# A transformer block on one core: the first half's attention begins in the product stage, and three additions change their engine

## The chip, the core and the metric

The kernel runs on one core of a Trainium2 chip. A core has several engines that run side by side, each strictly in the order of its own program: TensorE (PE, matrix products, with PEld for the loading of its weights), VectorE (DVE), ScalarE (ACT), GpSimd (POOL), and SyncE (SP), whose queue issues the transfers (DMA) between main memory and the on-chip memory SBUF. PE writes its results into PSUM, from where DVE and ACT take them. The metric is the time of one execution in microseconds of the device, as the median of several runs.

## The reference

The block adds three things: the input, a local attention on its layer norm, and a dense layer pair with the Mish function on the same layer norm. There are 2048 tokens of width 576, 32 heads of width 18, a window of 8 keys at a distance of 2 tokens each, and a hidden width of 4608.

```python
def block(x, wqkv, wo, w1, b1, w2):          # S=2048, D=576, F=4608, H=32, Dh=18
    xn = layernorm(x)
    q, k, v = split_heads(xn @ wqkv)
    idx = pos[:, None] - 2 * arange(8)[None, :]        # keys at t, t-2, ..., t-14
    logits = einsum("bhsd,bhswd->bhsw", q, k[idx]) * Dh ** -0.5
    attn = softmax(where(idx >= 0, logits, -1e9))
    o = einsum("bhsw,bhswd->bhsd", attn, v[idx])
    h = xn @ w1 + b1
    return x + o @ wo + (h * tanh(softplus(h))) @ w2
```

## The kernel before

The tokens are worked on in two halves of 1024 (hf = 0 and 1). Every operand of a matrix product is split into a high part and a low part (a cast, then a subtraction), and each product is three matmuls: high by high, high by low and low by high. Weights and activations also go through sums and differences of blocks, so that seven block products do the work of eight (names such as T1 to T4, S1 to S4, B11 to B22, P1 to P7 are such blocks and products).

The order of PE is written out as a list of items, called the plan; an item's position in it is its slot. The first half runs: the first part of the query, key and value products (items `q`, matmuls L540), then the rest of them in seven-product form (items `y`, L649, slots 20 to 32), then 18 quads of the dense layers: `m` items (L902 and L908: hidden layer h, blocks c11, c21, c22) and `p` items (L1004: second layer, added by DVE into `acc`, L1008). The second half has the items `v` and `z` (L649) in the place of `y`, then quads whose second layer is in part a seven-product scheme (L1096; its activations u are sums of stored blocks, its weights pw are fetched by `p_fetch`, L1064; DVE adds PSUM into accP, L1102, and `p_join`, L1105, joins two such sums), in part direct (L1117, with DVE's additions L1120). At the end come the items `o`, the product with wo (L1300).

All other work is put into slots by `before(slot, fn)`, and the engines' own order follows from it. Four tables correct this placing: `MOVED` moves the n-th call of `before` by some slots, to before or behind the item's own work; `STEPS` has the slots of the attention's steps, for each half; `SUMS` puts certain reductions of the attention into slots of their own; `AHEAD` names slots whose held Mish work runs first.

The attention of a half is a generator, eight rounds of two units (of two heads each). A round: POOL multiplies queries and keys (`pr`, L764, two instructions of 128x576 for each of four parts), DVE reduces each part to logits L (L769), DVE and ACT do the softmax (the exponential with a load of ACT's function table, L790; Mish, L948, uses another table), POOL multiplies with the values (`pv`, L803), DVE reduces (`og`, L809) and transposes (oT, L830), and SP stores the result (o_d, L839). Keys, values and queries are read back from main memory (kv_d, q_d) by `load_kv` and `load_kq`: the generator issues the first loads 4 slots ahead of the first step of the first half.

Tiles of one tag share a number of buffers. The tag `kv` has four: the key and value tiles of the attention, and in the stage `y` also the queries that this stage collects. A tile can be written only when the last reader of the buffer's former tile is done.

For the first product with wo, POOL forms the sums T3, T1, T2 and T4 (`wo_sum`, L1243, T2 from T1, T4 from T2), ACT casts their high parts and DVE subtracts (L1201, tiles raw_T and woh_T) for the low parts of T3, T1 and T2.

Of the kernel before, what the change touches and what calls it, by code (L numbers as in the profile page):

```python
# [12 lines left out]
ALU = mybir.AluOpType  # L13
# [22 lines left out]
MOVED = {0: (-1, 1),  # L36
 38: (-2, 1),
 41: (0, 0),
 47: (2, 1),
 49: (-2, 1),  # L40
 98: (-1, 1),
 108: (2, 0),
 117: (1, 0),
 118: (0, 0),
 121: (-2, 0),
 122: (1, 1),
 123: (0, 1, 0),
 126: (0, 1, 0),
 128: (0, 0),
 131: (0, 1, 0),  # L50
 135: (0, 1, 0),
 138: (0, 0),
 143: (0, 0),
 144: (0, 0),
 217: (0, 0),
 234: (0, 0),
 238: (-2, 1),
 282: (0, 0),
 345: (0, 0),
 378: (1, 1),  # L60
 389: (1, 0),
 400: (0, 0),
 413: (1, 1),
 416: (0, 0),
 421: (-1, 1),
# [3 lines left out]
 433: (0, 0),  # L69
 442: (2, 1),  # L70
 446: (0, 0),
 447: (0, 0),
 452: (-1, 1),
 465: (2, 1),
 468: (1, 1),
 481: (0, 1, 0),
 489: (0, 0),
 529: (0, 0),
 535: (0, 0),
 609: (1, 0),  # L80
 611: (0, 1, 0),
 614: (-1, 1, 0),
 618: (-2, 0),
 622: (-1, 1),
 625: (1, 1),
# [4 lines left out]
 662: (-2, 1),  # L90
 671: (2, 1),
 694: (1, 1),
 695: (-2, 1),
 737: (-1, 1),
 765: (2, 1),
 771: (1, 1),
 777: (1, 1),
 794: (0, 0),
 802: (0, 0),
 806: (0, 0),  # L100
 811: (-2, 0),
 834: (0, 0),
# [9 lines left out]
 1006: (0, 0),  # L112
 1042: (0, 0),
 1046: (2, 1),
 1056: (0, 1, 0),
 1057: (0, 0),
 1068: (0, 0),
 1070: (-2, 0),
 1086: (2, 1),
 1095: (1, 1),  # L120
 1101: (2, 1),
 1104: (2, 1),
 1106: (0, 0),
 1107: (2, 1),
 1116: (0, 0),
 1121: (0, 0),
 1122: (1, 0),
 1160: (-2, 1),
 1161: (-3, 1),
 1164: (1, 1),  # L130
 1166: (-2, 1),
 1201: (0, 1, 0),
 1207: (0, 0),
 1208: (0, 0),
 1212: (-2, 1),
 1219: (2, 1),
 1221: (1, 1),
# [5 lines left out]
 1237: (0, 0),  # L143
 1248: (0, 0),
 1249: (0, 0),
 1250: (0, 0),
 1251: (-2, 1),
 1253: (0, 0),
 1263: (2, 1),
 1266: (-2, 1),  # L150
 1274: (0, 1, 0),
 1292: (0, 0),
 1298: (1, 1),
 1336: (0, 0),
# [4 lines left out]
STEPS = ((33, 36, 47, 49, 53, 57, 63, 67, 70, 77, 78, 83, 85, 91, 95, 98, 105, 107, 111, 117, 123, 127, 130, 137, 139, 143,  # L159
# [7 lines left out]
SUMS = {(0, 0): (42, 1),  # L167
 (0, 1): (38, 0),
 (0, 11): (86, 0),
 (0, 15): (101, 0),  # L170
 (0, 17): (110, 0),
 (0, 32): (171, 0),
 (0, 34): (176, 0),
 (0, 36): (180, 0),
 (0, 37): (186, 0),
 (0, 38): (190, 0),
 (0, 47): (213, 1),
 (0, 50): (230, 0),
 (0, 53): (233, 1),
 (1, 2): (259, 1),  # L180
 (1, 5): (264, 0),
 (1, 6): (267, 0),
 (1, 8): (273, 0),
 (1, 10): (276, 0),
 (1, 28): (321, 0),
 (1, 35): (337, 0),
 (1, 38): (343, 0),
 (1, 46): (366, 0),
 (1, 47): (371, 0),
 (1, 50): (379, 1),  # L190
 (1, 54): (389, 0),
 (1, 56): (394, 1)}
AHEAD = (35, 37, 39, 42, 80, 84, 171, 184, 190, 191, 201, 218, 230, 231, 232, 237, 238, 240, 298, 315, 317, 336, 337, 357,
 391, 413, 414)
# [7 lines left out]
def block_kernel(ctx: ExitStack, tc: tile.TileContext, x, wq, wo, w1, b1, w2, mask, out):  # L202
# [1042 lines left out]
    def wo_src(name):  # L1245
        return (traw if name[0] == "T" else wraw)[name]
# [603 lines left out]
```

## Time and profile before

| quantity | us |
|---|---|
| median of 3 runs | 1100.46 |
| lowest and highest run | 1099.98, 1100.76 |
| the profiled execution | 1099.32 |
| its span, first to last instruction | 1097.5 |
| PE busy | 1085.5 |
| DVE busy | 883.8 |
| POOL busy | 789.6 |
| ACT busy | 512.8 |

All durations come from the one profiled execution, whose own time stands 1.14 us below the median. Of the rows that are shown later: a row of the stretches has the bounds in us, then the busy time and count of PE, PEld, DVE, ACT and POOL, the granted clock of PE, the busy share of the DMA engines, and GB/s. A row of the timeline has start and length in us, then engine, line, operation and tiles (output <- inputs), shapes and count; in brackets the idle time before it and what ended it. A row of the waits has who waited for what: us in all, times, the longest. A row of a line has the shortest, median and longest duration in ns, and the first and last start. In the chain of work that ended last, a row has start and length of one piece.

### The profile page before, as it was taken

Reading aid. Unit: us, or ns where it says so; the run is one execution under the profiler, and the core shown is the slowest. Engines: PE = TensorE matmul, PEld = TensorE weight load, DVE = VectorE, ACT = ScalarE, POOL = GpSimd, SP = SyncE. Lnnn points to the kernel's source line nnn. Section 1 sums busy time; section 2 is a strip of 40 time slices with the busy share of each in tenths; the row PEclk is TensorE's granted clock in tenths of the full one; section 3 lists DMA queues with packets and bytes.
Section 4 is the critical chain, followed back from the end, with each engine's and each line's share of the span. In section 5 each row is a group of like instructions: output and inputs, shape, how many; then the busy total and the mean of one; then the engine's idle time right before and its main releaser. Section 6 shows DMA issues by size and latency. Waiting matters only on the chain.

```text
span 1097.5 us, 18210 instructions
## 1 busy us (share of the span) xinstructions
PE 1085.5 (99%) x6454; PEld 999.2 (91%) x6454; DVE 883.8 (81%) x1469; ACT 512.8 (47%) x947; POOL 789.6 (72%) x635
## 2 busy tenths in 40 slices
PE   9999999999999999999999999999999999989998
PEld 8998899999999999999999888989999999979998
DVE  6775888898888889997976758887887885787886
ACT  5554564454456445455523354444444334244353
POOL 2435867778777787977777768778676799967432
PEclk9999999999999999999999999999999999999999
DMA  6769986877877588785799999675668576487864
GB/s 226 277 229 376 368 309 241 281 252 261 275 248 257 205 293 295 278 299 161 274 298 335 303 346 338 240 239 202 213 219 265 169 245 219 156 305 248 245 221 139
DMA packets 187327, 283.99 MB, mean 259 GB/s; under 512 B 53826, under 2 KB 127844, under 8 KB 187236
## 3 DMA queue, kind: packets, MB, share of 16 engines
q1 hardware_dynamic: 187236, 282.82, 76.0%
q8 instruction: 51, 0.84, 0.3%
q14 instruction: 40, 0.33, 0.1%
HBM read 166.58 MB, written 116.19 MB: 258 GB/s over the span
## 4 chain that ended last, share of the span: by engine, by line
PE 92%; DMA 3%; DVE 2%; issue 1%; ACT 1%; POOL 0%; POOLq 0%; SPq 0%
PE h L902 29%; PE po L1004 21%; PE po L1096 11%; PE po L1117 7%; PE h L908 5%; PE o L1300 5%; PE pq L540 3%; PE y L649 2%; PE z L649 2%; PE v L649 2%; PE zT L649 1%; PE yT L649 1%; DMA pw<-kept_B 1%; DMA pw<-kept_T 1%; DMA vw_T<-kept_vT 1%
## 5 line engine op out<-in xcount | busy, mean ns | idle before, releaser
L1004 PEld LDWEIGHTS po<-w,act 128*128 128x128 f32 x1728 | 236.1, 188 | 6.4 <-DVE acc L1008 1.0
L1004 PE MATMUL po<-w,act 128*128 128x288 f32 x1728 | 240.8, 295 | 0.6 <-DVE acc L1008 0.6
L803 POOL TENSOR_TENSOR pv<-L,kv 128x576 f32<-128x576 f32 x128 | 172.0, 1450 | 42.3 <-DVE L L796 19.8
L764 POOL TENSOR_TENSOR pr<-q,kv 128x576 f32<-128x576 f32 x128 | 195.0, 1552 | 1.9 <-DVE L L769 1.0
L954 POOL TENSOR_TENSOR act<-c,act 128x512 fp32r<-128x512 f32 x69 | 94.5, 1370 | 79.6 <-ACT act L953 78.6
L1096 PEld LDWEIGHTS po<-pw,u 128*128 128x128 f32 x1008 | 137.8, 188 | 6.1 <-issue 2.5
L1096 PE MATMUL po<-pw,u 128*128 128x288 f32 x1008 | 141.0, 295 | 1.3 <-ACT rt L936 0.7
L1008 DVE TENSOR_TENSOR acc<-po,acc 128x288 f32<-128x288 f32 x288 | 117.1, 448 | 18.9 <-PE po L1004 17.3
L902 PE MATMUL h<-xt,t 128*128 128x512 f32 x432 | 111.0, 391 | 0.1
L902 PE MATMUL h<-S,t 128*128 128x512 f32 x432 | 110.6, 391 | 0.1
L948 ACT ACTIVATE c<-c,b1c 128x512 f32<-128x512 f32 x69 | 50.0, 725 | 122.4 <-DVE c L947 122.3
L902 PE MATMUL h<-xt,wa 128*128 128x512 f32 x432 | 104.0, 389 | 0.0
L809 DVE TENSOR_REDUCE og<-pv 128x144 f32<-128x1152 f32 x64 | 86.1, 1345 | 19.6 <-POOL pv L803 19.6
L769 DVE TENSOR_REDUCE L<-pr 128x64 f32<-128x1152 f32 x64 | 85.7, 1341 | 15.7 <-POOL pr L764 15.7
L902 PEld LDWEIGHTS h<-xt,wa 128*128 128x128 f32 x432 | 80.9, 188 | 16.8 <-DMA wa<-kept_wa 0.3
L902 PEld LDWEIGHTS h<-xt,t 128*128 128x128 f32 x432 | 79.0, 188 | 15.4 <-DVE t L450 0.5
L902 PEld LDWEIGHTS h<-S,t 128*128 128x128 f32 x432 | 77.9, 188 | 13.8 <-ACT rm L936 0.4
L1117 PEld LDWEIGHTS po<-w,act 128*128 128x128 f32 x576 | 78.3, 188 | 5.2 <-DVE accP L1120 3.7
L1117 PE MATMUL po<-w,act 128*128 128x288 f32 x576 | 79.6, 295 | 3.3 <-DVE accP L1120 3.3
L1102 DVE TENSOR_TENSOR accP<-po,accP 128x288 f32<-128x288 f32 x156 | 63.2, 448 | 15.9 <-PE po L1096 7.9
L936 ACT COPY c<-h 128x512 f32<-128x512 f32 x69 | 40.4, 586 | 73.0 <-PE h L908 36.9
L947 DVE TENSOR_TENSOR c<-h,c 128x512 f32<-128x512 f32 x69 | 47.1, 683 | 23.9 <-PE h L908 20.7
(305 smaller groups left out, 2081.3 us busy)
## 6 DMA issues: line engine op xcount, KB each, us to landing
kv<-kv_d SPq DMA_DIRECT2D x64, 396.0 KB, 6.1
kept_t<-t SPq DMA_DIRECT2D x36, 512.0 KB, 5.0
t<-kept_t SPq DMA_DIRECT2D x36, 512.0 KB, 4.7
pw<-kept_T SPq DMA_DIRECT2D x24, 576.0 KB, 5.9
rw<-in_w SPq DMA_DIRECT2D x36, 320.0 KB, 5.1
kept_wa<-wa SPq DMA_DIRECT2D x18, 640.0 KB, 4.7
wa<-kept_wa SPq DMA_DIRECT2D x18, 640.0 KB, 7.4
rw<-in_w SPq DMA_DIRECT2D x36, 288.0 KB, 4.5
```

What stands on the lines that cost most here:

```text
L649: nc.tensor.matmul(h, l, r_, start=i == 0 and name in ("B11", "B21", "T3"), stop=i == len(seq) - 1, skip_group_check=True)
L764: nc.gpsimd.tensor_tensor(out=pr[:, x:x + hh], in0=q[:, j0 + x:j0 + x + hh, None, :].to_broadcast([P, hh, W, CU]), in1=win(kt, 0, CU, j0 + ...
L769: nc.vector.tensor_reduce(L[:, k, j0:j0 + hj].rearrange("p j w h -> p (j w h)"), pr.rearrange("p j w (h d) -> p (j w h) d", h=2), axis=AX, ...
L803: nc.gpsimd.tensor_tensor(out=pr[:, x:x + hj].rearrange("p j d w -> p j w d"), in0=L[:, k, x:x + hj, :, h:h + 1].to_broadcast([P, hj, W, DH]),
L809: nc.vector.tensor_reduce(og[:, c0:c0 + DH, :].rearrange("p d j -> p j d"), pr, axis=AX, op=ALU.add)
L902: nc.tensor.matmul(ph, wt[:, wl, wk * P:(wk + 1) * P], X[:, xs, :], start=first and i == 0, stop=last and i == len(seq) - 1, skip_group_ch ...
L954: nc.gpsimd.tensor_tensor(out=a[:, 1, :], in0=t, in1=a[:, 0, :].bitcast(F32), op=ALU.subtract)
L1004: nc.tensor.matmul(po, acts[hf, q, b, j][:, al, tok], done["w2", hf, 2 * q + j][:, wl, c * HC:(c + 1) * HC], start=i == 0, stop=i == 5)
L1008: nc.vector.tensor_tensor(out=t, in0=po, in1=t, op=ALU.add)
L1096: nc.tensor.matmul(po, units[e, k, qq][:, al, tok], w[:, qq, wl, :], start=i == 0, stop=i == 5)
L1102: nc.vector.tensor_tensor(out=t, in0=po, in1=t, op=ALU.add)
L1117: nc.tensor.matmul(po, acts[hf, q, b, j][:, al, tok], done["w2", hf, 2 * q + j][:, wl, c * HC:(c + 1) * HC], start=i == 0, stop=i == 5)
```

## The change

It has four parts.

1. The queries that the stage `y` collects lie in other buffers: two of them in one tile of tag `wa0`, the other two in tags `xn` and `acc`. The four `kv` buffers are free in that stage. `reserve` keeps only `wa1` for the first quad's weights and the tile for those queries.
2. The first half's attention has its first step in slot 26 (in the stage `y`) where it was slot 33, and its last in slot 252 where it was 251.
3. Three operations of POOL are done by DVE: the join P7 += P6 of the first part (`p_join`), and the differences T3 and T2 (`wo_sum`).
4. `MOVED`, `STEPS`, `SUMS` and `AHEAD` have new numbers, in both halves: loads, casts, subtractions, stores and reductions are moved by some slots. PE's own instructions and their order are as before.

```diff
-STEPS = ((33, 36, 47, 49, 53, 57, 63, 67, 70, 77, 78, 83, 85, 91, 95, 98, 105, 107, 111, 117, 123, 127, 130, 137, 139, 143,
+STEPS = ((26, 27, 29, 31, 34, 40, 45, 49, 56, 58, 63, 67, 72, 77, 80, 86, 90, 95, 99, 107, 110, 113, 120, 125, 129, 134, 139,
...
@@ -399,8 +473,8 @@
     def reserve():
-        for i in range(2):
-            early[f"wa{(i + 1) % 2}"] = sb.tile([P, 2, 5 * P], F32R, tag=f"wa{(i + 1) % 2}", bufs=1, name=f"wa_0_{i}")
+        early["wa1"] = sb.tile([P, 2, 5 * P], F32R, tag="wa1", bufs=1, name="wa_0_0")
+        early["qs"] = sb.tile([P, 2, 5 * P], F32, tag="wa0", bufs=1, name="qs_y0")
...
@@ -626,8 +700,13 @@
             if hf:
                 qs = sb.tile([P, 5 * P], F32, tag="xn", bufs=XNB, name=f"qs_{n_}")
+            elif g == 0:
+                if b == 0:
+                    yq["qs"] = early.pop("qs") if "qs" in early else sb.tile([P, 2, 5 * P], F32, tag="wa0", bufs=1, name=f"qs_{n_}")
+                qs = yq["qs"][:, b]
             else:
-                qs = sb.tile([P, (TJ + HALO) * CU], F32, tag="kv", bufs=4, name=f"qs_{n_}")
+                tag = ("xn", "acc")[b]
+                qs = sb.tile([P, (5 * P, D)[b]], F32, tag=tag, bufs=BUFS[tag], name=f"qs_{n_}")
...
@@ -1102,7 +1181,8 @@
     def p_join(a, b, pr):
-        nc.gpsimd.tensor_tensor(out=pacc[a, pr], in0=pacc[a, pr], in1=pacc[b, pr], op=ALU.add)
+        eng = nc.vector if (a, pr) == ("P7", 0) else nc.gpsimd
+        eng.tensor_tensor(out=pacc[a, pr], in0=pacc[a, pr], in1=pacc[b, pr], op=ALU.add)
...
@@ -1240,7 +1320,8 @@
         name, x, y = (("T3", "B22", "B12"), ("T1", "B12", "B11"), ("T2", "B22", "T1"), ("T4", "B21", "T2"))[n]
-        nc.gpsimd.tensor_tensor(out=traw[name], in0=wo_src(x), in1=wo_src(y), op=ALU.subtract)
+        eng = nc.vector if name in ("T3", "T2") else nc.gpsimd
+        eng.tensor_tensor(out=traw[name], in0=wo_src(x), in1=wo_src(y), op=ALU.subtract)
```

The line numbers of the kernel after are some 74 to 81 higher than those before. What the tables do to an engine's order is seen at the following places. A row has line, operation, output <- inputs (a number at a name's end only counts tiles) and the shape; x2 stands for two alike.

DVE in the second half, between the additions of quad 12's and quad 13's second layer (accP <- po, accP), before:

```order
L1120 TENSOR_TENSOR accP3_1_7610<-po_1_12_0_1_1_0_10640,accP3_1_7610 128x288
L1120 TENSOR_TENSOR accP3_1_7610<-po_1_12_0_1_1_1_10648,accP3_1_7610 128x288
L809 TENSOR_REDUCE og_1_5_10491<-pv_1_5_0_1_10564 128x8x18
L947 TENSOR_TENSOR c11_1_14_10673<-h2_1_14_10675,c11_1_14_10673 128x512
L1120 TENSOR_TENSOR accP4_0_7605<-po_1_13_1_0_0_0_10707,accP4_0_7605 128x288
L1120 TENSOR_TENSOR accP4_0_7605<-po_1_13_1_0_0_1_10715,accP4_0_7605 128x288
L1120 TENSOR_TENSOR accP5_0_7607<-po_1_13_1_0_1_0_10723,accP5_0_7607 128x288
L1120 TENSOR_TENSOR accP5_0_7607<-po_1_13_1_0_1_1_10731,accP5_0_7607 128x288
L809 TENSOR_REDUCE og_1_5_10491<-pv_1_5_1_0_10689 128x8x18
```

and after:

```order
L1200 TENSOR_TENSOR accP3_1_7583<-po_1_12_0_1_1_0_10639,accP3_1_7583 128x288
L1200 TENSOR_TENSOR accP3_1_7583<-po_1_12_0_1_1_1_10647,accP3_1_7583 128x288
L1324 TENSOR_TENSOR raw_T3_10660<-rB22_10608,rB12_10444 128x576
L888 TENSOR_REDUCE og_1_5_10490<-pv_1_5_0_1_10563 128x8x18
L1026 TENSOR_TENSOR c11_1_14_10672<-h2_1_14_10674,c11_1_14_10672 128x512
L1200 TENSOR_TENSOR accP4_0_7578<-po_1_13_1_0_0_0_10706,accP4_0_7578 128x288
L1200 TENSOR_TENSOR accP4_0_7578<-po_1_13_1_0_0_1_10714,accP4_0_7578 128x288
L1200 TENSOR_TENSOR accP5_0_7580<-po_1_13_1_0_1_0_10722,accP5_0_7580 128x288
L1200 TENSOR_TENSOR accP5_0_7580<-po_1_13_1_0_1_1_10730,accP5_0_7580 128x288
L888 TENSOR_REDUCE og_1_5_10490<-pv_1_5_1_0_10688 128x8x18
L1324 TENSOR_TENSOR raw_T2_10662<-rB22_10608,raw_T1_10661 128x576
```

The difference T3 (rB22, rB12: blocks of wo) now stands ahead of the reduction `og`, and T2 behind the next one, ahead of the additions that follow it.

DVE a quad later, where the low parts of T3 and T1 are formed, before:

```order
L1120 TENSOR_TENSOR accP3_1_7610<-po_1_13_0_1_1_1_10894,accP3_1_7610 128x288
L769 TENSOR_REDUCE L_1_6_10785<-pr_1_6_0_1_10849 128x64
L1201 TENSOR_TENSOR raw_T3_10661<-raw_T3_10661,woh_T3_10863 128x576
L1201 TENSOR_TENSOR raw_T1_10662<-raw_T1_10662,woh_T1_10923 128x576
L947 TENSOR_TENSOR c11_1_15_10936<-h2_1_15_10938,c11_1_15_10936 128x512
L769 TENSOR_REDUCE L_1_6_10785<-pr_1_6_1_0_10903 128x64
```

and after:

```order
L1200 TENSOR_TENSOR accP3_1_7583<-po_1_13_0_1_1_1_10893,accP3_1_7583 128x288
L1281 TENSOR_TENSOR raw_T3_10660<-raw_T3_10660,woh_T3_10862 128x576
L848 TENSOR_REDUCE L_1_6_10784<-pr_1_6_0_1_10848 128x64
L1281 TENSOR_TENSOR raw_T1_10661<-raw_T1_10661,woh_T1_10947 128x576
L1026 TENSOR_TENSOR c11_1_15_10935<-h2_1_15_10937,c11_1_15_10935 128x512
L848 TENSOR_REDUCE L_1_6_10784<-pr_1_6_1_0_10901 128x64
```

The low part of T3 moves ahead of a reduction of logits; that of T1 stands behind it.

POOL in the stage `y`, where the sums tt of the first quads' w1 (loaded as rw1) are formed, before:

```order
L435 TENSOR_TENSOR tt0_0_1073<-rw1_1_979,rw1_0_977 128x256
L435 TENSOR_TENSOR tt1_0_1074<-rw1_1_979 128x256
L435 TENSOR_TENSOR tt0_0_1073<-rw1_1_979,tt0_0_1073 128x256
L435 TENSOR_TENSOR tt1_0_1074<-rw1_0_977,tt0_0_1073 128x256
L435 TENSOR_TENSOR tt0_1_1177<-rw1_3_1119,rw1_2_1117 128x256
L435 TENSOR_TENSOR tt1_1_1178<-rw1_3_1119 128x256
L435 TENSOR_TENSOR tt0_1_1177<-rw1_3_1119,tt0_1_1177 128x256
L435 TENSOR_TENSOR tt1_1_1178<-rw1_2_1117,tt0_1_1177 128x256
L764 TENSOR_TENSOR pr_0_0_0_0_1210<-q_0_0_1082,kv0_0_0_1080 128x576 x2
L764 TENSOR_TENSOR pr_0_0_0_1_1264<-q_0_0_1082,kv0_0_0_1080 128x576 x2
```

and after:

```order
L843 TENSOR_TENSOR pr_0_0_0_0_1009<-q_0_0_900,kv0_0_0_898 128x576 x2
L843 TENSOR_TENSOR pr_0_0_0_1_1035<-q_0_0_900,kv0_0_0_898 128x576 x2
L509 TENSOR_TENSOR tt0_0_1092<-rw1_1_983,rw1_0_981 128x256
L509 TENSOR_TENSOR tt1_0_1093<-rw1_1_983 128x256
L509 TENSOR_TENSOR tt0_0_1092<-rw1_1_983,tt0_0_1092 128x256
L509 TENSOR_TENSOR tt1_0_1093<-rw1_0_981,tt0_0_1092 128x256
L843 TENSOR_TENSOR pr_0_0_1_0_1099<-q_0_1_904,kv0_0_1_902 128x576 x2
L843 TENSOR_TENSOR pr_0_0_1_1_1161<-q_0_1_904,kv0_0_1_902 128x576 x2
L509 TENSOR_TENSOR tt0_1_1196<-rw1_3_1131,rw1_2_1129 128x256
L509 TENSOR_TENSOR tt1_1_1197<-rw1_3_1131 128x256
```

The first four of the attention's products (x2 each) now stand ahead of and between the sums.

Two further places are told in words. At the end of the first half's products the reduction of L from pr_0_5_1_0 and a subtraction of the other half's layer norm stood on DVE right ahead of the additions into acc of the last quad; they now come behind those. On SP's queue, at the fetches pw of the last seven-product group, pw_5_2 stood ahead of the fetches w2_1_26, wa_1_14, w2_1_27, wc_1_14 and kv1_1_10, and these ahead of pw_5_3; now these five come first, then pw_5_2, the stores of oT, t0_1_14 and pw_5_3. The tiles w2 and pw share four buffers: pw_5_2 now takes that of pw_5_0, which is free when PE is done with it, and w2_1_27 the one that pw_5_2 had. Ahead of the fetch vw_T1 of the item v, two zacc loads (blocks of the kept y weights for the item z) go earlier on SP's queue, and one such pair more comes ahead of the fetch's second part.

More of the change, by code (lines that the diff above doesn't have):

```diff
@@ L77 @@
  489: (0, 0),
+ 499: (-1, 1),
+ 503: (0, 0),
+ 512: (1, 1),
+ 513: (1, 1),
+ 521: (0, 1, 0),
  529: (0, 0),
+ 533: (1, 1),
  535: (0, 0),
+ 545: (1, 1),
+ 565: (0, 0),
+ 603: (-1, 1),
  609: (1, 0),
  611: (0, 1, 0),
- 614: (-1, 1, 0),
- 618: (-2, 0),
+ 614: (-1, 1),
+ 617: (-2, 1),
+ 619: (0, 1, 0),
  622: (-1, 1),
- 625: (1, 1),
+ 623: (-2, 1),
+ 624: (-2, 1),
  627: (2, 1),
@@ L89 @@
  652: (-1, 1),
- 662: (-2, 1),
+ 662: (-2, 0),
  671: (2, 1),
+ 682: (2, 1),
+ 684: (0, 1, 0),
+ 685: (-2, 1),
  694: (1, 1),
  695: (-2, 1),
- 737: (-1, 1),
- 765: (2, 1),
+ 737: (1, 1),
+ 750: (2, 1),
  771: (1, 1),
  777: (1, 1),
+ 782: (0, 1, 0),
+ 787: (0, 1, 0),
+ 791: (0, 0),
+ 793: (0, 0),
  794: (0, 0),
  802: (0, 0),
+ 803: (1, 1),
+ 805: (2, 1),
  806: (0, 0),
+ 810: (-1, 1),
  811: (-2, 0),
+ 812: (0, 1, 0),
  834: (0, 0),
```

137 lines of the change are left out of this document (95 added, 42 removed), and 11 rows, old and new, of the table STEPS.

## The prediction

> **What bounds the kernel now.** I began with the span and clock of the core and the busy times, then asked what TensorE (PE) waits for, then read stretches of the span side by side.
>
> ```profile
> core 0: 1097.5 us, clock 1.000
> PE 1085.5 (99%) x6454; PEld 999.2 (91%) x6454; DVE 883.8 (81%) x1469; ACT 512.8 (47%) x947; POOL 789.6 (72%) x635
> ```
>
> PE is busy for 99% at full clock, and the change leaves its instructions and their order alone. So the time can fall only by PE's waits, and it rises wherever PE must wait anew. The list of PE's waits, longest first:
>
> ```profile
> PE po L1117 <- DVE accP L1120: 3.3, 1, 3.3
> PE warm L227 <- POOL ident masks.py:199: 1.3, 1, 1.3
> PE v L649 <- DMA vw_T<-kept_vT: 1.1, 1, 1.1
> PE po L1096 <- ACT rt L936: 0.7, 1, 0.7
> PE po L1096 <- DMA pw<-kept_T: 0.6, 1, 0.6
> PE po L1004 <- DVE acc L1008: 0.6, 1, 0.6
> ```
>
> Each happens once. The warm start is before anything that changes. By stretches (PE, PEld, DVE, ACT, POOL busy):
>
> ```profile
> 75.00:100.00 25.00, 25.00 (x126) 23.22 (x125) 11.78 (x26) 10.07 (x26) 5.69 (x7) 1.00 1.05 350
> 125.00:500.00 375.00, 375.00 (x2271) 343.56 (x2270) 331.37 (x524) 191.78 (x310) 294.87 (x245) 1.00 0.78 271
> 500.00:600.00 100.00, 98.37 (x574) 93.34 (x574) 78.33 (x135) 42.32 (x106) 75.41 (x64) 1.00 0.82 267
> 600.00:700.00 100.00, 99.21 (x529) 87.19 (x528) 71.36 (x102) 44.05 (x80) 75.20 (x55) 1.00 0.95 318
> 880.00:905.00 25.00, 24.41 (x158) 22.61 (x157) 22.26 (x35) 8.32 (x14) 24.07 (x17) 1.00 0.78 245
> 905.00:940.00 35.00, 35.00 (x221) 32.49 (x221) 20.25 (x39) 13.49 (x20) 34.15 (x28) 1.00 0.60 216
> 940.00:965.00 25.00, 21.73 (x129) 19.44 (x128) 20.94 (x23) 8.87 (x15) 21.63 (x17) 1.00 0.52 146
> ```
>
> In the first half's products (125 to 500 us) PE never stops: nothing is to be gained there, only lost. PE's idle time in the four stretches where it stops is 1.63 + 0.79 + 0.59 + 3.27 = 6.28 us, and that is the most that can come back. Over half of it is one wait, from 960.8 to 964.06 us. What POOL, DVE and PE did there:
>
> ```profile
> 953.58 2.90 POOL L764 TENSOR_TENSOR pr<-q,kv 128x576 f32<-128x576 f32 x2
> 957.60 2.90 POOL L764 TENSOR_TENSOR pr<-q,kv 128x576 f32<-128x576 f32 x2
> 963.86 1.29 POOL L954 TENSOR_TENSOR act<-c,act 128x512 fp32r<-128x512 f32 x1 [3.37 <-ACT act L953]
> ...
> 952.48 1.35 DVE L769 TENSOR_REDUCE L<-pr 128x64 f32<-128x1152 f32 x1 [2.10 <-POOL pr L764]
> 953.75 8.03 DVE L1201 TENSOR_TENSOR raw_T<-raw_T,woh_T 128x576 fp32r<-128x576 f32 x2
> 961.70 0.68 DVE L947 TENSOR_TENSOR c<-h,c 128x512 f32<-128x512 f32 x1
> 963.56 1.53 DVE L1120 TENSOR_TENSOR accP<-po,accP 128x288 f32<-128x288 f32 x4
> ...
> 964.06 2.23 PE L1117 MATMUL po<-w,act 128*128 128x288 f32 x15 [3.27 <-DVE accP L1120]
> L1201 DVE TENSOR_TENSOR raw_T<-raw_T,woh_T x4: 744/1256/7362, 953.7 to 974.7; 128x576 fp32r<-128x576 f32 x4
> ```
>
> The pair of L1201 took 8.03 us, the one of them 7.362 us where the shortest of that line took 0.744. Its two inputs lie in SBUF, as POOL's do, and it ended just after POOL fell idle, at 957.60 + 2.90 = 960.50. So DVE was kept out for 6.6 us while POOL ran instruction after instruction; behind it stood the accP additions that empty PSUM for PE. POOL itself is the cause: 34.15 of 35 us busy before 940.
>
> **The change, part by part.** *Three additions go from POOL to DVE* (the P7 join and the differences T3 and T2). T3 and T2 come off POOL in its full stretch:
>
> ```profile
> L1243 POOL TENSOR_TENSOR raw_T<-rB,rB x2: 1448/1456/1465, 931.2 to 936.2; 128x576 f32<-128x576 f32 x2
> L1243 POOL TENSOR_TENSOR raw_T<-rB,raw_T x2: 1517/1520/1524, 941.3 to 946.9; 128x576 f32<-128x576 f32 x2
> 910.27 0.46 DVE L1120 TENSOR_TENSOR accP<-po,accP 128x288 f32<-128x288 f32 x1 [2.53 <-PE po L1117]
> 928.03 1.35 DVE L809 TENSOR_REDUCE og<-pv 128x144 f32<-128x1152 f32 x1
> 930.91 0.69 DVE L947 TENSOR_TENSOR c<-h,c 128x512 f32<-128x512 f32 x1 [1.53 <-PE h L908]
> 937.53 0.46 DVE L1120 TENSOR_TENSOR accP<-po,accP 128x288 f32<-128x288 f32 x1 [0.44 <-PE po L1117]
> ```
>
> POOL loses T3 (1.45) and T2 (1.52), and a join of the same size (about 1.45, an estimate from these): 4.4 us. DVE gains three instructions that no row shows on it. The nearest row is L1201: same shape and two inputs in SBUF, 0.744 at best, 1.256 the median, 7.362 at worst. I take 1.3 each. The join stands ahead of the 2.53 us gap before 910.27, T3 ahead of the reduce of 928.03 and so of the 1.53 us gap before 930.91: both are covered. T2 stands behind the next og reduce and right before the accP additions of 937.53, where the gap is 0.44, so those run about 0.9 us late. PE has room for that: of the 6.6 us for which DVE was held up at 953.75, PE paid 3.27, so the first 3.3 us of such a delay were free. T2 also waits for T1 on POOL, which two removed instructions bring forward. Cost of the three on PE: 0, from 0 to the starvation priced below.
>
> The gain is the 3.27 at 960.8. With 4.4 us less ahead of it POOL is done with its row of pr products earlier, but I do not expect it to idle much before: its rows carry over 3 us of backlog (3.37 of idle came only once ACT was the one waited for). What decides is whether the L1201 addition gets its turn; in the changed order it comes right after a group of accP additions, ahead of the reduce that was before it. The bounds are 0 (kept out until POOL idles, as before) and 3.27; I take 3.0, since of the line's four instructions half took no more than 1.256, and with such a turn DVE is through well before PE needs it.
>
> The Trainium skill, "SBUF — State Buffer", section "SBUF: two separate sides", says that DVE with two SBUF inputs and GpSimd share a port pair as an exclusive lock, held for one whole instruction by whoever starts first. By that rule DVE would wait for one POOL instruction, some 1.5 us, then run; the whole 3.27 comes back, and the sum below would be -4.6 in place of -4.3. The trace differs: 7.362 us spans five POOL instructions, so the row decides.
>
> *The attention of the first half begins in slot 26, not 33*, with the query buffers moved so that its loads can go out in that stage. What it meets there:
>
> ```profile
> 84.59 0.88 POOL L435 TENSOR_TENSOR tt<-rw,rw 128x256 f32<-128x256 f32 x1 [16.46 <-DMA rw<-in_w]
> 80.86 0.46 DVE L654 TENSOR_TENSOR kvs_y<-yT,kvs_y 128x288 f32<-128x288 f32 x1 [6.05 <-PE yT L649]
> L769 DVE TENSOR_REDUCE L<-pr 128x64 f32<-128x1152 f32 x64 | 85.7, 1341 | 15.7 <-POOL pr L764 15.7
> L764 POOL TENSOR_TENSOR pr<-q,kv x128: 1412/1437/1965, 101.2 to 1003.9; 128x576 f32<-128x576 f32 x128
> L790 ACT ACT_TABLE_LOAD  x13: 1283/1283/1283, 143.6 to 1009.2; - x13
> ```
>
> Eight pr products are 8 x 1.44 = 11.5 us on POOL. Four now stand ahead of the tt sums of 84.59, in a gap of 16.46; the rest follow where 75 to 100 has 19.3 us free. Of four reduces (4 x 1.34 = 5.4 us) the first have the 6.05 us gap before 80.86. The four loads go out 7 slots earlier on SP's queue, ahead of a stretch where the DMA share is 1.05. What isn't covered is ACT: the table load of the exponential (1.283; the first was at 143.6) and the load back now come among the copies and the Mish of the first quad. Bounds 0 and 2 x 1.28 = 2.6; I take +0.5, as ACT is busy for only 10.07 of 25 us just before. Attention steps spread over 227 slots instead of 219 take work from ahead of the tight additions later: 0, since PE does not wait there.
>
> *The table of places.* Near 526 and 567:
>
> ```profile
> 523.27 1.34 DVE L769 TENSOR_REDUCE L<-pr 128x64 f32<-128x1152 f32 x1
> 526.21 1.06 PE L1004 MATMUL po<-w,act 128*128 128x288 f32 x6 [0.56 <-DVE acc L1008]
> 560.49 6.35 DMA vw_T<-kept_vT
> 882.27 6.39 DMA pw<-kept_T
> 888.79 3.41 PE L1096 MATMUL po<-pw,u 128*128 128x288 f32 x24 [0.59 <-DMA pw<-kept_T]
> ```
>
> The reduce of 523.27 (1.34) moves behind the acc additions that PE waits 0.56 for: -0.56. On SP two zacc loads go ahead into its free time, one pair more goes ahead of the vw_T load issued at 560.49: its 1.07 falls by something between 0 and 1.07; -0.6. In return a cast and the exponential stand ahead of copies that PE takes up at once: 0 to 1.28 by the table load, +0.4. Sum -0.8. Between 600 and 700 two loads and a POOL product are put in another order: of the 0.79 I take half, -0.4. Before 888.79 five transfers leave SP's queue ahead of the pw load that took 6.39 from its issue at 882.27 to its landing: -0.6. The pw load before it now gets the buffer of the group's first item, and has the length of the second (3.41, as the one of 888.79) and what lies between to land in: 0 to 3.0 by a landing of 6.39, and I take 0, as those five are no longer in its way.
>
> Sum: -3.0 + 0.5 - 0.8 - 0.4 - 0.6 = -4.3 us. The profiled execution took 1099.32, so 1095.0 of its kind; the median, 1100.46, stands 1.14 above it, and so 1096.1 is forecast.
>
> **The rivals.**
> 1. *The addition is kept out again.* POOL's backlog survives the loss of 4.4 us, as its row without gaps suggests, and L1201 waits until POOL idles: the 3.0 does not come, 1100.46 - 1.3 = 1099.2. Against it: it is one row of four.
> 2. *The moved additions are kept out* (slower). T2 and T3 are of L1201's kind and stand in POOL's fullest stretch. Kept out for 6.6, T2 makes the accP additions of 937.53 about 6.2 late; 6.6 late cost PE 3.3 at 960.8, so about 3.0 here, T3 some 1.5 after its gaps. With rival 1's wait kept as well: 1100.46 - 1.3 + 4.5 = 1103.7. It decides from two of the three up.
> 3. *Attention is ahead of tight additions in the first half* (slower). A reduce of 1.34 ahead of a c addition in six of fifteen quads, PE having no idle time to absorb it, gives 6 x 1.34 = 8.0: 1096.1 + 8.0 = 1104.1. Against it: the order puts fewer reduces there, not more.
> 4. *The small waits stay or only change place*, the large one goes, with the table loads at their bound: 1100.46 - 3.0 + 2.0 = 1099.5.
>
> **How the numbers follow.** No change within 0.2%, 2.2 us, could be told from none. Forecast 0.56 (its own range 1094 to 1098), rival 1 0.17, rival 2 0.09, rival 3 0.09, rival 4 0.09. Forecast is faster; rivals 1 and 4 lie mostly within 0.2%, with 0.06 of their 0.26 faster; rivals 2 and 3 are slower. Faster 0.62, same 0.20, slower 0.18. If all 6.28 us came back and nothing was lost the time would be 1094.2; less the spread of the runs (1099.98 to 1100.76), 1093.4. Upward the range takes in rivals 1 and 4 and the lower part of 2: 1102.5.
>
> **What would show it.** Right: no PE wait for accP of over 1 us near 960, L1201's longest under 2 us; the three new additions under 2 us each; PE full from 125 to 500; no waits at 526 and 888. Wrong: a DVE addition of 5 us or more between 905 and 960; PE waits for h, c or act between 95 and 130; a wait of PE for ACT copies near 559.

## The result and the profile after

The changed kernel takes 1091.98 us (median of 5 runs, 1091.35 to 1092.42) where the kernel before takes 1100.76 (median of 5 runs beside them, 1099.98 to 1102.89): a ratio of 0.9918, with an interval of 0.9903 to 0.9932. That is 8.8 us, twice the 4.4 forecast, and 1.4 us under the range. The profiled execution of after took 1092.39, with a span of 1090.6, so 6.9 us less than the profiled one of before. Three executions among those below took 1326, 1389 and 2944 us; ratios and counts of executions leave them out. Core and busy times, then PE's waits:

```profile
core 0: 1090.6 us, clock 1.000
PE 1083.0 (99%) x6454; PEld 998.4 (92%) x6454; DVE 901.0 (83%) x1472; ACT 513.3 (47%) x947; POOL 787.9 (72%) x632
```

```profile
PE warm L301 <- POOL ident masks.py:199: 1.3, 1, 1.3
...
PE po L1197 <- DVE accP L1200: 0.6, 1, 0.6
PE h L981 <- ACT c L1015: 0.4, 1, 0.4
PE h L981 <- DVE c L1026: 0.3, 1, 0.3
```

The waits for vw_T, rt, pw and acc are gone, and that for accP is 0.6 where it was 3.3. Two waits for c are new. The same stretches as before (bounds, then PE, PEld, DVE, ACT, POOL, granted clock, DMA share, GB/s):

```profile
125.00:500.00 375.00, 375.00 (x2271) 343.68 (x2270) 328.06 (x519) 191.86 (x311) 288.75 (x242) 1.00 0.78 270
500.00:600.00 100.00, 99.92 (x582) 94.86 (x581) 79.38 (x136) 42.30 (x106) 76.90 (x65) 1.00 0.83 274
600.00:700.00 100.00, 100.00 (x545) 89.53 (x545) 76.59 (x109) 43.42 (x80) 75.89 (x57) 1.00 0.92 311
880.00:905.00 25.00, 25.00 (x161) 23.36 (x160) 22.42 (x35) 9.65 (x17) 23.33 (x16) 1.00 0.59 207
905.00:940.00 35.00, 34.40 (x218) 31.73 (x217) 26.36 (x37) 10.99 (x17) 30.03 (x24) 1.00 0.59 213
940.00:965.00 25.00, 24.70 (x151) 22.45 (x150) 21.66 (x36) 12.37 (x18) 21.18 (x16) 1.00 0.78 253
```

Only the two stretches from 905 on lack more than 0.1 us. What DVE, POOL and PE did there, in the order of the timeline:

```profile
923.26 6.01 DVE L1324 TENSOR_TENSOR raw_T<-rB,rB 128x576 f32<-128x576 f32 x1
929.20 1.34 DVE L888 TENSOR_REDUCE og<-pv 128x144 f32<-128x1152 f32 x1
930.46 0.68 DVE L1026 TENSOR_TENSOR c<-h,c 128x512 f32<-128x512 f32 x1
...
926.27 2.50 POOL L882 TENSOR_TENSOR pv<-L,kv 128x576 f32<-128x576 f32 x2
932.67 1.30 POOL L1033 TENSOR_TENSOR act<-c,act 128x512 fp32r<-128x512 f32 x1 [3.90 <-ACT act L1032]
...
937.54 3.44 PE L1197 MATMUL po<-w,act 128*128 128x288 f32 x24 [0.60 <-DVE accP L1200]
941.28 1.65 PE L981 MATMUL h<-xt,t 128*128 128x512 f32 x6 [0.30 <-DVE c L1026]
```

The difference T3, now on DVE, was kept out for 6.01 us, as L1201 was before. It got through when POOL had run dry, at 926.27 + 2.50 = 928.77, and POOL was dry because the c addition (930.46) that its next Mish product needs stood behind T3. The low parts, which cost 3.3 us before, got through, and the PE group that had waited until 964.06 starts without a wait:

```profile
L1281 DVE TENSOR_TENSOR raw_T<-raw_T,woh_T x4: 744/1262/1897, 947.0 to 967.3; 128x576 fp32r<-128x576 f32 x4
957.31 3.34 PE L1197 MATMUL po<-w,act 128*128 128x288 f32 x24
```

PE issues the same instructions in the same order in both kernels, so the start of one can be set against its start in the other. How much earlier (-) or later (+) the changed kernel is by some places of before, in us:

| at, in before | shift | added since the row above | forecast |
|---|---|---|---|
| 100 | +0.19 | +0.19 | 0 |
| 125 | +0.56 | +0.37 | +0.5 |
| 500 | +0.41 | -0.15 | 0 |
| 600 | -1.32 | -1.73 | -0.8 |
| 700 | -3.78 | -2.46 | -0.4 |
| 880 | -3.94 | -0.16 | 0 |
| 905 | -4.77 | -0.83 | -0.6 |
| 950 | -3.32 | +1.45 | 0 |
| 970 | -6.88 | -3.56 | -3.0 |
| end | -6.93 | -0.05 | 0 |

Not every row is the work of the change: the shift between 600 and 700 comes, nearly whole, in two kernels below that change nothing there (see Nine).

Each wait that went gave more than its idle time, as at 657 us. PE there, before and then after:

```profile
655.47 0.61 PE L908 MATMUL h<-xt,wc 128*128 128x512 f32 x2
656.75 3.44 PE L1096 MATMUL po<-pw,u 128*128 128x288 f32 x24 [0.67 <-ACT rt L936]
660.03 1.54 PE L902 MATMUL h<-xt,t 128*128 128x512 f32 x6
```

```profile
653.64 0.61 PE L987 MATMUL h<-xt,wc 128*128 128x512 f32 x2
654.09 3.33 PE L1175 MATMUL po<-pw,u 128*128 128x288 f32 x24
657.26 1.53 PE L981 MATMUL h<-xt,t 128*128 128x512 f32 x6
```

From the start of the first row to that of the second it is 1.28 before and 0.45 after, 0.83 less for an idle time of 0.67, and the group that follows takes 0.11 less. In the same way the waits of 0.56, 1.07, 0.59 and 3.27 us moved the starts by 0.81, 1.23, 0.75 and 3.43.

### The profile page after: what moved, and what is told of

The parts are those of the page before. It is cut to its first block, busy times and chain, and to the rows that moved or that the text cites. A ratio compares the mean times of both kernels' runs of the same rounds, so it can differ in the third digit from the quotient of the medians.

```text
span 1090.6 us, 18209 instructions
## 1 busy us (share of the span) xinstructions
PE 1083.0 (99%) x6454; PEld 998.4 (92%) x6454; DVE 901.0 (83%) x1472; ACT 513.3 (47%) x947; POOL 787.9 (72%) x632
```

## The experiments

The kernels run on several chips, each beside before on its own chip; the ratios are to that. MOVED, STEPS, SUMS and AHEAD are the tables of places; the changed MOVED differs from the old in 114 calls, of which a diff below shows one or two.

**One: the three additions on VectorE alone, in before.**

```diff
-        nc.gpsimd.tensor_tensor(out=traw[name], in0=wo_src(x), in1=wo_src(y), op=ALU.subtract)
+        eng = nc.vector if name in ("T3", "T2") else nc.gpsimd
+        eng.tensor_tensor(out=traw[name], in0=wo_src(x), in1=wo_src(y), op=ALU.subtract)
...
-        nc.gpsimd.tensor_tensor(out=pacc[a, pr], in0=pacc[a, pr], in1=pacc[b, pr], op=ALU.add)
+        eng = nc.vector if (a, pr) == ("P7", 0) else nc.gpsimd
+        eng.tensor_tensor(out=pacc[a, pr], in0=pacc[a, pr], in1=pacc[b, pr], op=ALU.add)
```

> The kernel before, with only the three operations (P7 join, T3, T2) on DVE; tables, buffers and attention as before. Theory A (DVE with two inputs in SBUF is kept out as long as POOL runs on without a pause): POOL has 4.4 us less work ahead of 953, so either the L1201 addition gets its turn (under 2 us) or one of the new DVE operations is kept out in its place; PE's 3.3 us wait near 960 becomes at most 1.5: the time falls by 1.8 to 3.4 us, to about 1097.4 to 1099 where before takes 1100.8. Theory B (the wait at 960 is cured by the new places alone, and the engine of the three does not matter): the 7.4 us addition and the 3.3 us wait stay, time within 1 us of before.

1097.95 us (10 runs), ratio 0.9976 (0.9959 to 0.9993). The time and PE's wait of 1.0 us are those of Theory A, but not its mechanism: the low part is kept out as long as before (7.3 us), only from an earlier start on, and the new T3 and T2 got through (0.75 and 1.07). The timeline, then the list of waits:

```profile
950.63 7.97 DVE L1202 TENSOR_TENSOR raw_T<-raw_T,woh_T 128x576 fp32r<-128x576 f32 x2
```

```profile
PE po L1118 <- DVE accP L1121: 1.0, 1, 1.0
```

**Two: the three additions back on GpSimd, in the changed kernel** (the diff of One in reverse).

> The kernel after, with the three operations back on POOL; all else as after. Theory A: POOL has no pause from 905 to 957 again, an L1281 addition is kept out for 4 us or more, PE waits 2 to 3.4 us for accP near 955, while the 6.0 us T3 on DVE and its two PE waits (0.76 and 0.46) are gone: 1 to 2.2 us slower than after, about 1093 to 1094. Theory B: no addition over 2 us, and without T3's waits 1.2 us faster than after, about 1090.8.

1092.24 us (4 runs), ratio 0.9916 (0.9886 to 0.9945): with the new places the engine of these additions makes no difference to the time that these runs could tell. Neither theory had it: the low part is kept out here too, against B, and PE hardly waits, against A (DVE and PE in the timeline):

```profile
945.46 6.80 DVE L1280 TENSOR_TENSOR raw_T<-raw_T,woh_T 128x576 fp32r<-128x576 f32 x1
...
956.46 1.71 PE L1196 MATMUL po<-w,act 128*128 128x288 f32 x11 [0.51 <-DVE accP L1199]
```

Here it begins 10.5 us ahead of the time at which PE is ready for that group (956.46 - 0.51 - 945.46). In before that is 7.0 (960.8 - 953.75) and PE waits 3.3, in One 9.2 and PE waits 1.0. So being kept out for 7 us is paid for by the time that is missing to some 10 to 11 us; the place takes the wait away, and a lighter POOL takes a part of it only as it lets the addition begin earlier. Whether the low part is kept out goes with the engine: with the new places and T2 on DVE (after, Four, Ten, Eleven, Thirteen, Fourteen) no low part took over 1.9 us, with all three on POOL (here and in Five) one took 6.8. To PE that is worth the 0.5.

**Three: two low parts left out, in before.**

```diff
+        if name in ("T3", "T1"):
+            return
         h, src = whi[name]
         nc.vector.tensor_tensor(out=src.bitcast(F32R), in0=src, in1=h.bitcast(F32), op=ALU.subtract)
```

> The kernel before, with the two L1201 subtractions of T3 and T1 left out (the low part stored is then the raw sum, so two subtractions of the computation are missing). Theory A: no DVE instruction with two SBUF inputs is in the way at 953, PE's 3.3 us wait for accP goes, and the time falls by 3.3 us (1097.5 where before takes 1100.8). If DVE was late at 960 for another reason (its order, or the reductions waiting for POOL), a wait of 1 us or more stays and the time falls by less than 2 us.

1096.43 us (10 runs), ratio 0.9955 (0.994 to 0.997): the wait at 964 is gone (-3.43 in PE's starts), no DVE operation takes more than 1.98 us. The wait was these additions' alone.

**Four: T3 with one input, in the changed kernel** (the block B12 left out of it).

```diff
+        if name == "T3":
+            nc.vector.tensor_reduce(traw[name], wo_src(x)[:, :, :, None], axis=AX, op=ALU.add)
+            return
         eng = nc.vector if name in ("T3", "T2") else nc.gpsimd
```

> The kernel after, with T3 on DVE formed from one SBUF input (a reduction over an axis of length one, which copies block B22; the subtraction of B12 is left out). Theory A: with one input it is not kept out, so it takes under 1.5 us where the subtraction took 6.0, and the two PE waits behind it (0.76 and 0.46) go: 1.2 us faster than after, about 1090.8. If it was the place or a wait of its own that held it, it takes 6 us again and the time is that of after.

1091.81 us (5 runs), ratio 0.9919. The profiled execution was the longest of them, 1095.86. The timeline of DVE and PE in it, then the stretch after the wait:

```profile
923.14 0.74 DVE L1324 TENSOR_REDUCE raw_T<-rB 128x576 f32<-128x576 f32 x1
...
932.12 7.55 DVE L1327 TENSOR_TENSOR raw_T<-rB,raw_T 128x576 f32<-128x576 f32 x1
...
940.10 4.89 PE L1197 MATMUL po<-w,act 128*128 128x288 f32 x24 [3.28 <-DVE accP L1200]
```

```profile
940.00:944.00 4.00, 3.90 (x18) 3.90 (x19) 3.97 (x8) 0.18 (x1) 1.22 (x1) 0.59 0.00 0
```

With one input T3 was through in 0.74 us, with POOL at work beside it as in the profile of after, where it took 6.01. By itself that could be chance, since T3 with two inputs also got through in Eleven, Thirteen and Fourteen (1.07 to 1.08). All sixteen profiles together settle it: no DVE instruction with one input was more than 0.12 us longer than the shortest of its form, and of the additions with one input in PSUM those into acc and accP stayed within 0.46 and those into c within 0.69; every longer delay is one with two inputs in SBUF. T2, with two inputs, was then kept out for 7.55 until POOL paused at 939.1, and PE waited 3.28. This is what the prediction's second rival has for T2, in one execution. The PE group after the wait took 4.89 us where its like takes 3.34, at a granted clock of 0.59: of this more below.

**Five: only the places from slot 350 on, in before.** Engines, buffers and the rest of the tables, the attention's steps too, as before.

```diff
 MOVED = {
- 737: (-1, 1),
+ 737: (1, 1),
+ 750: (2, 1),
...
- 1336: (0, 0),
```

> The kernel before, with only the changed places of slots 350 and later (second half, about 850 us on); the three operations stay on POOL, the attention's start and all earlier places are as before. Theory P (the wait at 960 is a matter of where DVE's long addition stands: an addition is still kept out for 6 to 7 us, but from an earlier point, when PE does not need DVE): the long addition stays, PE's wait near 960 falls from 3.3 to about 0.5 as with the three operations put back, and that at 888 goes: 3.3 us faster, about 1096.5 where before takes 1099.8. Theory A (the lighter POOL cures it): POOL is as full as before, PE's wait near 960 stays above 2.5 us; only 0.6 to 0.8 us faster.

1097.01 us (5 runs), ratio 0.9958 (0.994 to 0.9976). The wait at 889 is gone (-0.75), and that at 964 is 0.5 (the line's durations, then the wait):

```profile
L1201 DVE TENSOR_TENSOR raw_T<-raw_T,woh_T x4: 743/1262/6808, 950.8 to 972.5; 128x576 fp32r<-128x576 f32 x4
```

```profile
PE po L1117 <- DVE accP L1120: 0.5, 1, 0.5
```

Still kept out for 6.8 us, but from 950.8 on, ahead of a reduction and not behind it. POOL has all its work here, so a lighter POOL is not needed for it.

**Six: the first half's part alone, in before** (buffers, early start, places up to slot 253).

```diff
-STEPS = ((33, 36, 47, 49, 53, 57,
+STEPS = ((26, 27, 29, 31, 34, 40,
...
-        for i in range(2):
-            early[f"wa{(i + 1) % 2}"] = sb.tile([P, 2, 5 * P], F32R, tag=f"wa{(i + 1) % 2}", bufs=1, name=f"wa_0_{i}")
+        early["wa1"] = sb.tile([P, 2, 5 * P], F32R, tag="wa1", bufs=1, name="wa_0_0")
+        early["qs"] = sb.tile([P, 2, 5 * P], F32, tag="wa0", bufs=1, name="qs_y0")
```

> The kernel before, with the new query buffers, the attention's earlier start and the changed places of the slots up to 253; the rest as before. By the trace after, place by place: +0.5 us at the first quad (114 us), then -0.8, -0.2 and -0.2 at the end of the products and -1.2 at the vw_T load, so about -1.8 near 600 us; the waits at 656, 888 and 960 stay as before. Time about 1.8 us below before. If the gains near 526 and 567 came from chance in the transfers, the waits there come back: about +0.5.

1097.30 us (10 runs), ratio 0.9972 (0.996 to 0.9985). PE's starts: +0.54 at 114, -0.81 at 526, -1.24 at 567; the wait of 3.3 at 964 stays. The profile still ends 0.34 later than that of before, with waits of 0.73 for pw at 660 and 0.80 for an activation u at 728, and a low clock from 960 to 968 (0.84 and 0.73).

**Seven: the places of slots 254 to 299, in before** (about 600 to 700 us). The steps of the second half's attention are all those of the changed kernel, so that four of them in slots 357 to 366 (near 880 us) move by a slot as well.

```diff
 MOVED = {
- 765: (2, 1),
+ 782: (0, 1, 0),
+ 787: (0, 1, 0),
```

> The kernel before, with only the changed places of slots 254 to 299 (about 600 to 700 us). The trace after gains 1.9 us there, which the prediction put at 0.4. If the places do it, PE's waits at 656, 662 and 676 go and the time falls by 1.4 to 1.9 us, the rest as before; if it takes the earlier work of the first half, less than 0.7.

1101.42 us (10 runs), ratio 1.0007 (0.9992 to 1.0021), so no change. In the profile PE's starts gain 2.4 us between 600 and 700, as in the changed kernel, but others add to them: +0.47 at 567, where nothing was changed; +0.88 at 883, where DVE has a reduction of L ahead of an addition that stood before it, and -0.75 at 889, where the wait of before is gone; and a longer wait at 963 with the clock low behind it (of that more under Twelve):

```profile
600.00:700.00 100.00, 100.00 (x543) 89.55 (x543) 76.31 (x106) 43.19 (x80) 76.77 (x58) 1.00 0.95 319
960.00:964.00 4.00, 0.95 (x7) 0.95 (x8) 4.00 (x8) 2.55 (x5) 1.15 (x1) 1.00 0.74 227
964.00:968.00 4.00, 4.00 (x20) 4.00 (x19) 3.28 (x7) 1.55 (x2) 0.14 (x1) 0.57 0.95 300
```

**Eight: the early start with the old table of places, in before** (the diff of Six and the reductions' places, SUMS, of the first half; MOVED and AHEAD as before).

> The kernel before, with the new query buffers, the steps of the first half's attention from slot 26 on and its reductions in the new slots; all other places as before. Theory 1 (an earlier start has nothing to give in itself, since PE never waits between 125 and 500 us): the waits at 526, 567 and later stay, and in the first quads PE waits 0.4 us or more anew, up to several us where the old places do not fit the new steps: the same or slower, 0 to +4 us. Theory 2 (the earlier start is what frees the end of the products): the waits at 526 and 567 go, 1 to 2 us faster.

1117.35 us (4 runs), ratio 1.0152 (1.0123 to 1.0181): slower by some 17 us. PE's waits, and two stretches:

```profile
PE h L907 <- DVE c L952: 5.5, 3, 3.5
PE po L1009 <- DVE acc L1013: 3.3, 2, 2.2
...
PE h L907 <- DVE t L450: 2.7, 1, 2.7
```

```profile
116.00:120.00 4.00, 4.00 (x10) 3.13 (x11) 1.35 (x2) 1.95 (x4) 4.00 (x4) 0.50 1.01 405
...
308.00:312.00 4.00, 4.00 (x13) 3.32 (x12) 3.16 (x7) 1.33 (x3) 1.28 (x1) 0.50 1.04 381
```

DVE's additions for PE come late in the first half, which is the prediction's third rival, at twice its price. Without the new places the early start does harm.

**Nine: only the places of slots 207 to 253, in before** (about 500 to 600 us; buffers and start as before).

```diff
 MOVED = {
- 614: (-1, 1, 0),
- 618: (-2, 0),
+ 614: (-1, 1),
+ 617: (-2, 1),
+ 619: (0, 1, 0),
```

> The kernel before, with only the changed places, steps and reductions of slots 207 to 253 (about 520 to 600 us); the attention's start in slot 33 and the old query buffers stay. Theory 1 (the places there take PE's waits away; the early start gives nothing in itself): the wait at 526 (0.6) and that at 567 for vw_T (1.1 to 1.6) go and the one at 114 does not come: 2.0 us less by 600 us in the profile, time 1.5 to 2.5 us below before. Theory 2 (the early start is needed for them): one or both waits stay, less than 0.7 us gained.

1097.82 us (10 runs), ratio 0.9975 (0.9961 to 0.9988). -0.81 at 526 and -1.23 at 567, as in Six: these gains are the places', not the early start's. But PE's starts also gain 2.32 us between 600 and 700, where nothing was changed. One, whose three additions all lie behind 900 us, gains 2.31 there. That stretch in One, then in Nine:

```profile
600.00:700.00 100.00, 100.00 (x543) 89.67 (x542) 73.75 (x103) 45.17 (x83) 76.63 (x57) 1.00 0.95 321
```

```profile
600.00:700.00 100.00, 100.00 (x545) 89.47 (x544) 73.22 (x108) 44.56 (x81) 76.60 (x57) 1.00 0.92 309
```

Each of these changes is against the first profile of before. The other five with the old places of slots 254 to 299 lie between -0.53 (Six) and +0.63 (Eight), four of them with a wait of 0.7 to 1.6 us for the transfer pw at the place of 662; the eight with the new places between -0.81 (Eleven) and -2.46. So the new places make this gain more frequent, but an execution can have it without them.

**Ten: T3 back on GpSimd, in the changed kernel.**

```diff
-        eng = nc.vector if name in ("T3", "T2") else nc.gpsimd
+        eng = nc.vector if name in ("T2",) else nc.gpsimd
```

> The kernel after, with T3 on POOL again (P7 and T2 stay on DVE). If the 6.0 us T3 is what PE's two waits at 937 and 941 come from, they go and the time is up to 1.2 us below after, 1090.8; a later DVE subtraction that is kept out in its place (T2 or the low part of T3, as in three of the kernels run so far) would cost 0.5 to 3.3 again: between 1090.8 and 1094.

1091.94 us (11 runs), ratio 0.9936 (0.9916 to 0.9956): 7 runs near 1091.5, and 4 of 1098.0 to 1098.9, beyond the range that was expected, with a granted clock of 0.997 or 0.998 where the others have 0.999 or 1.000. The profile is of one of the short ones, has T2 at 2.90 us and no PE wait near 940; what happened in the long ones has no profile.

**Eleven and twelve: the two kernels once more, unchanged, on one chip.**

> The kernel after, unchanged, for a second profile and times beside the other runs of this call. If the addition that is kept out is fixed by the program, T3 takes 6.0 us again and PE waits 0.6 and 0.3 at the same places; if it is chance, it is another one or none, and the waits near 940 differ. Time 1092, with little spread.

1092.22 us (6 runs), ratio 0.9917 (0.99 to 0.9934). Now T3 got its turn, and it is POOL's product beside it that took 1.81 us in place of 1.28:

```profile
925.24 1.08 DVE L1324 TENSOR_TENSOR raw_T<-rB,rB 128x576 f32<-128x576 f32 x1
...
925.66 1.81 POOL L1033 TENSOR_TENSOR act<-mn,act 128x512 fp32r<-128x512 f32 x1
```

No wait of PE stands near 940 us. Whether T3 is kept out differs between profiled executions of the same program; whether the chip has a part in it is not shown.

> The kernel before, unchanged, for a second profile. The waits for DMA at 567, 656 to 663 and 888 should differ from those of the first profile by up to 1 us each (they did in the kernels that share these places), which is where its wide spread of times and the gain beyond the profile's 6.9 us would come from; L1201 at 953 takes 7.4 us again if it is fixed by the program. Ratio 1.000 to itself.

1099.98 us (10 runs), ratio 0.9989 (0.9974 to 1.0003). L1201 took 7.35 us again, and PE waited 3.31. The wait at 656 is absent here, and one of 1.2 for pw stands at 662. This profile has something that the first profile of before lacks. PE in the timeline, and the stretch after the wait:

```profile
964.41 4.98 PE L1117 MATMUL po<-w,act 128*128 128x288 f32 x24 [3.31 <-DVE accP L1120]
```

```profile
964.00:968.00 4.00, 3.59 (x15) 3.59 (x16) 3.93 (x9) 2.82 (x5) 1.28 (x1) 0.57 0.99 275
```

The stretch in the first profile of before, after the same wait:

```profile
964.00:968.00 4.00, 3.94 (x27) 3.84 (x28) 3.93 (x10) 2.55 (x4) 1.15 (x1) 1.00 1.00 275
```

Twenty-four matmuls took 4.98 us where they take 3.34 at full clock: 1.64 more, on top of the wait.

**Thirteen and fourteen: the changed kernel with the old beginning, and the changed kernel beside it.** The old buffers, the attention from slot 33 on and the old places below slot 207; all else as changed.

```diff
     def reserve():
-        early["wa1"] = sb.tile([P, 2, 5 * P], F32R, tag="wa1", bufs=1, name="wa_0_0")
-        early["qs"] = sb.tile([P, 2, 5 * P], F32, tag="wa0", bufs=1, name="qs_y0")
+        for i in range(2):
+            early[f"wa{(i + 1) % 2}"] = sb.tile([P, 2, 5 * P], F32R, tag=f"wa{(i + 1) % 2}", bufs=1, name=f"wa_0_{i}")
```

> The changed kernel with the first half's beginning put back: queries in the old buffers, attention from place 33 on as before, and the places below 207 those of before; every place from 207 on, and the three additions on VectorE, as changed. Nothing of the computation is left out. Theory P (the places of 500 us and after make the whole gain, and the early start gives none): the wait at 114 us for the first quad's copy (0.54 us) is absent, the rest is as in the changed kernel, and the time lies 0 to 0.9 us under that of the changed kernel run beside it. Rival E (the early start is what makes the new places possible, as room that they use): waits of 1 us and more return between 200 and 500 us, where the two orders meet, and the time is 2 us or more above the changed kernel's. The mean granted clock should be 1.000 in every execution by Theory P, since no PE wait of 3 us is left.

> The changed kernel once more, beside the kernel with the old beginning on the same chip. Both theories: 1091 to 1093 us, mean granted clock 1.000 in every execution. Of the subtraction T3 on VectorE (6014 ns in one profile of this kernel, 1076 ns in the other) it shows a third draw; if it is under 2 us, no PE wait of 0.4 us or more stands between 930 and 960 us.

1091.64 us (4 runs, 1091.06 to 1091.97), ratio 0.9915 (0.99 to 0.993), against 1091.22 (4 runs, 1090.77 to 1091.92), ratio 0.9912 (0.9896 to 0.9929). The two do not differ by anything that these runs can tell; the 0 to 0.9 us that Theory P gave to the old beginning are not seen. The wait of 0.5 at 114 is absent with the old beginning (-0.54 in PE's starts), and this execution has a wait of 0.5 for an activation u at 726, as that of Ten has. So the buffers and the early start carry no part of the gain that shows; it comes with the places from slot 207 on and the three additions, of which the latter add nothing that Two could tell. In the third profile of the changed kernel T3 took 1.07 us and PE was full from 905 to 965:

```profile
905.00:940.00 35.00, 35.00 (x225) 32.68 (x224) 23.85 (x42) 12.64 (x19) 33.96 (x26) 1.00 0.61 219
940.00:965.00 25.00, 25.00 (x153) 22.92 (x153) 19.06 (x33) 12.29 (x19) 19.09 (x14) 1.00 0.80 266
```

## Why the prediction was right and wrong

**Right.** The direction; that PE's waits carry the change; the wait at 964, its cause and its size (-3.56 against -3.0), by the addition's new place; +0.37 at the first quad against +0.5, the only cost of the early start; nothing lost from 125 to 500; -0.83 against -0.6 before 889. The first rival was half true: the low part can be kept out just as long (6.8 us in Two and Five), but it then no longer costs PE what it cost. What decided was when it begins, and not, as the prediction had it, whether it gets its turn.

**Wrong: "that is the most that can come back".** The 6.28 us were the sum of idle times in one execution, and three things lie outside it. First, a wait costs PE 0.16 to 0.25 us more than its idle column shows, by the five starts above. Second, small delays have no idle row at all: -0.21 at 534, -0.23 at 538, -0.22 at 662, -0.23 at 676. Third, the profiled execution was a fortunate one: it took 1099.32, and the prediction added the 1.14 us to the median as a surplus that the change leaves alone ("and so 1096.1 is forecast"). With the change the surplus went: after's profiled execution is longer than its median. With the five runs of each, the difference of the medians is 6.93 in the profiles, 1.44 by which the profile of before lies under their median, 0.41 by which the profile of after lies over its own, together 8.78.

What the surplus consists of is shown in part. One piece is the low clock after the wait of 3.3 us. Of 83 executions of before on the four chips, 9 have a mean granted clock of 1.000, as the profiled one had, 58 have 0.998 and 16 have 0.997; 0.43 of the clock lost for 4 of 1099 us is 0.0016, so most executions have such a stretch. All ten of One, where the wait is 1.0 us, have 1.000. Of the changed kernel's 15 executions 14 have 1.000 and one 0.999. The trace prices it at 1.6 us. Another piece is the waits for transfers, which change from one execution to the next: for vw_T at 567 they are 1.07, 0.6, 1.6 and 1.5 us in the first profile, Twelve, Five and Seven, and for pw at 662 up to 1.6 (Five). How the surplus divides between the two is open: of before and of Nine, both with the wait at 964, the executions at 1.000 are by their medians only 0.3 to 0.9 us shorter than those at 0.998 on the same chip where there were two or more of each, less than the trace's 1.6.

**Wrong: "of the 0.79 I take half, -0.4", and "-0.8" near 526 and 567.** They measured -2.46 and -1.73. Near 526 and 567 the term was too small: the prediction took about half of the wait at 567 and set +0.4 against it for copies near 559, where no wait came; both waits go, by 0.81 and 1.23 (Six, Nine, Thirteen). Between 600 and 700 taking half had no reason behind it either, but the -2.46 is in part the luck of the draw: One and Nine have as much without those places, and Seven, which has them, has no gain in its ten runs. What the new places are worth there stays open. The ratios of Five, Seven and Nine together give 0.6%, and all places from slot 207 on with the three additions 0.85% (Thirteen); with intervals of 0.13 to 0.18% on each of the four the runs cannot tell whether the parts add up.

**Wrong in the first profile, right in three others: the three additions on DVE at 0.** T3 was kept out for 6.01 us and cost 1.45, the price that the second rival had for it ("T3 some 1.5"); in Eleven, Thirteen and Fourteen it took 1.07 to 1.08 us and cost nothing. So this term is 0 or about 1.5 by chance, with a rare 3.3 and more if it is T2 (Four).

**The rule that was weighed.** The Trainium skill, "SBUF — State Buffer", section "SBUF: two separate sides", has the pair of ports locked for one whole instruction by whoever starts first. In Eleven the trace agrees: T3 waits and is through in 1.08, and POOL's next instruction is longer by 0.5. In the first profile of after, in One, Two, Four and Five it does not: 6.0 to 7.6 us span several POOL instructions. That it hits operations with two inputs in SBUF agrees with all sixteen profiles (under Four).

## What to carry to other kernels

The idle time of PE in one profile is no upper bound of what a change of places can bring: count every wait with its excess, ask what the clock does behind waits of some 3 us, and compare the profiled execution with the median before adding their difference to a forecast. A second profile of the unchanged kernel tells which waits are there every time. An operation that can be kept out for 7 us is cured by being started earlier, ahead of work that nobody waits for; moving its neighbours to another engine brought 0.24% with the old places, where it let the operation begin earlier, and nothing that showed with the new ones. And an early start of a stage is worth nothing by itself: with the old places it cost 17 us, and with the new ones it could be left out.

## What the hardware showed that I had not expected

**The clock after a wait.** After PE waits of 3.3 us in Four and Twelve, of 3.6 in Seven, and of 2.7 and 3.5 in Eight, the granted clock is 0.50 to 0.59 over a stretch of 4 us, as the fences of these show. In Eight a wait of 2.2 us is enough, with 24 matmuls of 4.97 us behind it that take 3.34 at full clock:

```profile
448.67 4.97 PE L1009 MATMUL po<-w,act 128*128 128x288 f32 x24 [2.19 <-DVE acc L1013]
```

After the 3.27 of the first profile of before it is 1.00, and no such stretch is in the profiles of the changed kernel, where no wait exceeds 1.3. The Trainium skill, "TensorE: Matmul & The Clock Gate", section "Part 1: The HAM clock gate (the "warmup" mystery)", says that the array drops to half clock after about one idle window of 3.4 us, that the window runs freely, and that about as long a busy stretch restores it. By that rule the loss is half of 3.4, an estimate of 1.7 us from that page; the trace has 1.64. That an equal wait goes with and without it agrees with a free-running window. But the waits of 2.2, 2.7 and 3.3 us are all shorter than the page's window; there the measurements decide.

**Kept out or not.** An addition of DVE with two inputs in SBUF took 1.1 or 6.0 us in the same program, beside the same work of POOL. In before the low part was kept out in both profiles, 7.36 and 7.35, and in the five other kernels with its old place (One, Six, Seven, Eight, Nine) for 7.30 to 7.38. What decides at the moment when POOL goes from one instruction to the next is open; no run here tells it.
